# Four-row issue of the second last block's turning transfers, and a later place for the combine weights, in a fused attention and soft-MoE kernel

## The chip, the cores and the metric

The kernel runs on one core of one Trainium2 chip. The metric is device time in microseconds of one execution. Before the change the median of three runs is 650.25 us (649.88 to 651.46). The engines are named as in the profile: PE is TensorE (matmuls; PEld its weight loads), DVE is VectorE, ACT is ScalarE, POOL is GpSimd, and SP is SyncE, which issues the DMA transfers.

## What is computed

The reference is three layers in a row, on 8 sequences of 576 tokens (4608 tokens in all, 512 channels):

```
# 1. attention with a decay per head, 8 heads of 64
scores = (q @ k.T) / 8
x = (scores * Dmat) @ v
# 2. feed-forward, 512 -> 2048 -> 512
h = x @ w_in
x = (h * sigmoid(1.702 * h)) @ w_out
# 3. soft mixture of experts, 8 experts of 4 slots
logits = x @ phi                      # 4608 x 32
d = softmax(logits over the tokens)
slot_input = d.T @ x                  # 32 x 512
slot_out[e] = relu(slot_input[e] @ w1[e]) @ w2[e]
c = softmax(logits over the slots)    # the combine weights
out = c @ slot_out
```

## The kernel before

**Tiling.** The tokens go through in 12 blocks of 384 (n = 0 to 11; LAST is 11). Each block's hidden layer is cut into 16 chunks of 128 (fc = 0 to 15). For one chunk, `expert_scores` (L368) makes the product hp of 12 matmuls; `gelu` (L378) on ScalarE writes the result gT, with the hidden channel on the partitions. The logits never pass through the second feed-forward product: w_out and phi are joined beforehand into Wp, and `logits_group` (L419) multiplies four chunks of gT by it.

**Turning.** The slots' sum needs gT with the token on the partitions. For blocks 0 to 10, VectorE transposes squares of 32 x 32 from gT into pre (L394). SyncE then issues 16 transfers, four rows of four, that put the squares in their places in nat (`shuffle`, L412), once for each half of a block's chunks. A transfer holds 96 KB, in pieces of 1 KB. nat exists once. Block 11 is turned by TensorE in place of this (tpg, L401).

**The softmax over tokens** runs block by block with a running maximum. For block n - 1 it is done during block n: `softmax_split` (L425, L426), `softmax_exp` (product lt, maximum, exponential on ScalarE, L432 to L452), `softmax_turn` (L461: three transposes on TensorE into dp; then VectorE copies dn, finds mx and writes Lall, L463 to L466), and `slots_part` (L479: the product Sg of dn and nat, 12 matmul instructions in the program, 24 in the trace; L485 adds it into acc). Of the twelve products the first two read the first half of nat, the third is the first that reads the second half, and it waits for all transfers of that half. dp stands in the PSUM buffer of tag L, of which there is one; the next block's logits product Lg takes the same buffer, so it waits until L466 has read dp.

**The combine weights.** Lall holds the logits less their maximum, for all tokens. `combine_part(0, NPRE)` takes the exponential of the first 30 of 36 token tiles on ScalarE (L489), and `combine_rest` normalises them with four VectorE instructions (L495 to L498). The other six tiles are done in the tail. The results are read only in the tail.

**The weights of the experts** (w1 and w2, 33.5 MB) and w_out are loaded ahead in the rooms of things that are no longer used: `prefetch` takes the next unit of a fixed list (512 or 1024 KB) and a room, and issues one transfer; `prefetch_three` cuts one room into 1024 and 512 KB. In block 11 a room of tag w (two chunks of w_in) is given away every second chunk, as soon as these chunks' hp product has read it.

**What sets the order.** Everything here is in a `manual_schedule`: each engine runs its instructions in the order in which the code issues them. All transfers stand on SyncE's one queue. They use eight semaphores in turn, so a transfer is issued only when the eighth before it has landed.

Of the kernel before, what the change touches and what calls it, by code (L numbers as in the profile page):

```python
# [9 lines left out]
F32 = mybir.dt.float32  # L10
F32R = mybir.dt.float32r
I32 = mybir.dt.int32
AF = mybir.ActivationFunctionType
# [66 lines left out]
NPRE = NTILE - 2 * NT128  # L80
# [53 lines left out]
def tile_kernel(ctx, tc, qkv, w_in, w_turned, w_out, phi, w1, w2, consts, out):  # L134
    nc = tc.nc
    pe, act, dve, pool, sp = nc.tensor, nc.scalar, nc.vector, nc.gpsimd, nc.sync
# [4 lines left out]
    pw = ctx.enter_context(tc.tile_pool(name="pw", bufs=NFC // 2 - 1, reuse_waits="tile"))  # L141
# [4 lines left out]
    pb = ctx.enter_context(tc.tile_pool(name="pb", bufs=1, side="right", reuse_waits="tile"))  # L146
# [18 lines left out]
    Lall = pp.tile([128, NTILE, NS], F32, name="Lall")  # L165
# [187 lines left out]
    gT, pre, nat, Lg, dn, Lps, dTs = {}, {}, {}, {}, {}, {}, {}  # L353
# [53 lines left out]
    def shuffle(n, hf, rows=range(4)):  # L407
        if n not in nat:
            nat[n] = pm.tile([128, NT128, 4, NFC, 32], F32, tag="nat", name="nat")
        for a in rows:  # L410
            for b in range(4):
                sp.dma_start(nat[n][32 * b:32 * b + 32, :, a, hf * HF:(hf + 1) * HF, :],  # L412
                             pre[n, hf][32 * a:32 * a + 32, :, b])

    def logits_group(n, g):
        if g == 0:
            Lg[n] = ps.tile([128, NB], F32, tag="L", name="Lg")
        for fl in range(GF):
# [38 lines left out]
    def softmax_turn(n):  # L457
        dT = dTs.pop(n)
        dp = ps.tile([128, NT128, 128], F32, tag="L", name="dp")
        for c in range(NT128):  # L460
            pe.transpose(dp[:, c, :], dT[:, c * 128:(c + 1) * 128], ident)  # L461
        dn[n] = pm.tile([128, NT128, NS], F32, tag="dn", name="dn")
        dve.tensor_copy(dn[n], dp[:, :, 0:NS])  # L463
        mx = pm.tile([128, NT128], F32, tag="mx", name="mx")
        dve.tensor_reduce(mx, dp[:, :, NS:2 * NS], axis=AX.X, op=ALU.max)
        dve.tensor_tensor(Lall[:, n * NT128:(n + 1) * NT128, :], dp[:, :, NS:2 * NS],  # L466
                          mx.unsqueeze(2).to_broadcast([128, NT128, NS]), op=ALU.subtract)
# [16 lines left out]
        else:  # L484
            dve.scalar_tensor_tensor(acc, acc, st["corr"], sg, op0=ALU.mult, op1=ALU.add)  # L485

    def combine_part(t0, t1):
        L = Lall[:, t0:t1]
        act.activation(L, L, AF.Exp)  # L489
        combine_rest(t0, t1)  # L490

    def combine_rest(t0, t1):
        L = Lall[:, t0:t1]
        s_ = csum[:, t0:t1]
        dve.tensor_reduce(s_, L, axis=AX.X, op=ALU.add)  # L495
        dve.tensor_scalar(s_, s_, 1e-9, None, op0=ALU.add)
        dve.reciprocal(s_, s_)
        dve.tensor_tensor(L, L, s_.unsqueeze(2).to_broadcast([128, t1 - t0, NS]), op=ALU.mult)  # L498
# [9 lines left out]
    wx, places = {}, []  # L508

    def place_in(pool_, tag, bufs, n=2):  # L510
        return lambda: pool_.tile([128, 1024 * n], F32, tag=tag, name="wx", bufs=bufs)
# [15 lines left out]
    def prefetch(place=None, n=2, lone=False):  # L527
        if not (todo or half_left):
            return
        if place is None:  # L530
            n, place, _ = places.pop(0)
        if lone:
            unit = next(u for u in todo if len(u) == 1)
            todo.remove(unit)
        elif n == 1 and half_left:
            unit = half_left.pop()
        elif n == 1:
            unit = todo.pop(0)
            if len(unit) == 2:
                half_left.append(unit[1:])  # L540
        else:
            pairs_ = [u for u in todo if len(u) == 2]
            unit = pairs_[0] if pairs_ else half_left.pop() if half_left else todo[0]
            if unit in todo:
                todo.remove(unit)
        load_unit(unit[:n], place)
        places.append((n, place, unit[:n]))

    def prefetch_three(t, single, lone=False):

        two = t[:, 1 - single // 2:3 - single // 2].rearrange("p a d -> p (a d)")
        for n in ((1, 2) if single == 0 else (2, 1)):
            prefetch((lambda: t[:, single]) if n == 1 else (lambda: two), n, lone and n == 1)
# [272 lines left out]
    with tc.manual_schedule(engines={getattr(mybir.EngineType, e) for e in ("PE", "Activation", "DVE", "Pool", "SP")}):  # L826
        for x in START:
            step(x)
        for n in range(2, LAST):
            early = n == LAST - 1  # L830
            step_at, logits_at, split_at, exp_at, turn_at, slots_at = (
                (EARLY_STEP_AT, EARLY_LOGITS_AT, EARLY_SPLIT_AT, EARLY_EXP_AT, EARLY_TURN_AT, EARLY_SLOTS_AT) if early else
                (STEP_AT if n < LAST - 2 else BEFORE_EARLY_STEP_AT, LOGITS_AT, SPLIT_AT, EXP_AT, TURN_AT, SLOTS_AT))
            for fc in range(NFC):
                main_fc(n, fc)
                for f in LATE_TURNS.get(fc, (fc,)) if n == 2 else (fc,):
                    turn_fc(n, f)
                if fc in KEEP_AT and n < 2 + NFC // 2 and wide:
                    keep_w_out(2 * (n - 2) + KEEP_AT[fc][0], KEEP_AT[fc][1])

                def between():
                    for m, k in logits_at.get(fc, ()):
                        logits_group(n - m, k)
                    if fc == split_at:
                        softmax_split(n - 1)

                if fc in step_at:
                    step_of((n + 1) * STEPS + step_at[fc], between)
                else:
                    between()  # L850
                if fc == (0 if early else min(step_at)) and (early or n == 2):
                    shuffle(n - 1, 1)
                if early and fc == 2:
                    prefetch(lambda: ring_raw[:, 0:4].rearrange("p a f -> p (a f)"))
                if early and fc == max(step_at):
                    att_ctx.close()
                    pw2 = ctx.enter_context(tc.tile_pool(name="pw2", bufs=NW2, side="right", reuse_waits="tile"))
                    for _ in range(NW2):
                        prefetch(place_in(pw2, "w", NW2))
                if fc == slots_at:  # L860
                    slots_part(n - 1)
                    shuffle(n, 0)
                if fc == exp_at:
                    softmax_exp(n - 1)
                if fc == turn_at:
                    softmax_turn(n - 1)
                if fc == NFC - 1 and not early:
                    if n < LAST - 2:
                        shuffle(n, 1)
                if fc == NFC - 1 and early:  # L870
                    prefetch_three(pb.tile([128, 3, 1024], F32, tag="x", name="wx", bufs=1), 2)
                    shuffle(n, 1)
                    prefetch_three(pb.tile([128, 3, 1024], F32, tag="pre", name="wx", bufs=2), 0)
                if n == 3 and fc == 0:
                    for unit, a in zip(kept, (4, 8)):
                        load_unit(unit, lambda a=a, n=len(unit): ring_raw[:, a:a + 2 * n].rearrange("p a f -> p (a f)"))
        n = LAST
        for fc in range(NFC):
            main_fc(n, fc)
            if fc in LAST_LOGITS:  # L880
                for m, g in LAST_LOGITS[fc]:
                    logits_group(n - m, g)
            if fc == 0:
                softmax_split(n - 1)
            if fc == LAST_EXP_AT:
                softmax_exp(n - 1)
                combine_part(0, NPRE)
            if fc == LAST_TURN_AT:
                softmax_turn(n - 1)
            if fc == LAST_SLOTS_AT:  # L890
                slots_part(n - 1)
            if fc == 5:
                prefetch_three(pb.tile([128, 3, 1024], F32, tag="pre", name="wx", bufs=2), 0, lone=True)
            for f in LAST_TURNS.get(fc, ()):
                turn_fc(n, f)
            if fc == 13:
                prefetch(lambda: gate_room[:, 1536:2560], 1)
            if fc == 0:
                prefetch(place_in(pw, "w1", 2, 1), 1)
            elif fc % 2 == 0:  # L900
                prefetch(place_in(pw, "w", NFC // 2 - 1))
            if fc == GF:
                gate()
                prefetch(lambda: gate_room[:, 0:1024], 1)
        tail()
# [47 lines left out]
```

## Time and profile before

| | us |
|---|---|
| median of three runs | 650.25 |
| the profiled execution's own time | 650.49 |
| its span, first to last instruction | 648.6 |
| TensorE busy | 626.7 (97%) |
| VectorE busy | 293.8 (45%) |
| ScalarE busy | 216.7 (33%) |

The span lies 1.9 us under the execution's own time. Block 10 ends near 532.5 us, block 11 runs from there to about 579, and the tail (the slots' experts and the combination) from there to the end. The granted clock of TensorE is at full speed throughout the blocks. A DMA share is the mean busy share of the core's 16 DMA engines; it can exceed 1 slightly, since packets overlap. A row of the timeline merges neighbouring instructions of one line. "to landing" is the time from a transfer's issue to the moment it is complete on all its engines; the view gives it for some of them.

### The profile page before, as it was taken

To read this page: it belongs to the slowest core of one execution; us is meant where nothing else is said; L and a number is where in the kernel's file an instruction comes from. 1 tells how busy PE (TensorE), PEld (TensorE's weight loads), DVE (VectorE), ACT (ScalarE), POOL (GpSimd) and SP (SyncE) were. 2 spreads that over 40 slices of the span, in tenths; PEclk is the share of its full clock that TensorE was granted. 3 is DMA by queue.
4 is the path that set the end of the run, shared out by engine and by line. 5 is a ranking of instruction groups with operands and counts; after the bars stand their busy time and mean duration, and the time that the engine had idled before them with its cause. 6 is when DMAs were issued, how large, how long until landed. Compare 5 with 4: busy or idle time off the path is not lost.

```text
span 648.6 us, 19162 instructions
## 1 busy us (share of the span) xinstructions
PE 626.7 (97%) x8439; PEld 538.0 (83%) x8439; DVE 293.8 (45%) x581; ACT 216.7 (33%) x409; POOL 77.6 (12%) x70
## 2 busy tenths in 40 slices
PE   6999999999999999999999999999999999999994
PEld 6898788898998989989989979989898798874562
DVE  4989933364453443454534534544535323123043
ACT  2765432141242232422412412412424224231042
POOL 2011101211112101121111011111121100001000
PEclk9999999999999999999999999999999999999997
DMA  8997657687676756746657657566566777999998
GB/s 337 404 329 267 256 109 218 164 215 187 174 265 165 195 187 163 211 141 180 172 163 182 183 145 187 170 158 179 179 176 190 251 204 209 413 361 421 412 414 353
DMA packets 62546, 150.64 MB, mean 232 GB/s; under 512 B 8192, under 2 KB 42368, under 8 KB 53248
## 3 DMA queue, kind: packets, MB, share of 16 engines
q1 hardware_dynamic: 62464, 149.43, 72.8%
q8 instruction: 66, 1.08, 0.7%
q14 instruction: 16, 0.13, 0.1%
HBM read 101.16 MB, written 13.63 MB: 177 GB/s over the span
## 4 chain that ended last, share of the span: by engine, by line
PE 87%; DMA 6%; DVE 3%; ACT 1%; issue 1%; POOL 0%; SPq 0%; DVEq 0%; ACTq 0%
PE hp L368 56%; PE Lg L419 5%; PE Sg L479 4%; PE Sp L227 4%; PE St L227 4%; DMA early_raw<-in_moe_w_in_dram 3%; PE Op L227 2%; PE h_ps L710 2%; PE op L787 2%; PE so_ps L761 1%; DMA early_raw<-in_w_turned_dram 1%; PE so_ps L753 1%; DMA ring<-in_w_turned_dram 1%; DMA pack<-in_qkv_dram 1%; PE tpg L401 1%
## 5 line engine op out<-in xcount | busy, mean ns | idle before, releaser
L368 PE MATMUL hp<-x,w 128*128 128x384 f32 x2304 | 420.0, 339 | 1.6 <-POOL x L257 1.3
L368 PEld LDWEIGHTS hp<-x,w 128*128 128x128 f32 x2304 | 397.4, 188 | 20.2 <-issue 15.7
L394 DVE STREAM_TRANSPOSE pre<-gT 128x384 f32<-128x384 f32 x172 | 95.3, 569 | 165.5 <-ACT gT L378 154.5
L378 ACT ACTIVATE gT<-hp 128x384 f32<-128x384 f32 x188 | 91.1, 490 | 232.6 <-PE hp L368 232.2
L257 POOL TENSOR_TENSOR x<-xs,x 128x512 fp32r<-128x512 f32 x33 | 42.5, 1288 | 310.6 <-ACT x L252 310.6
L227 PE MATMUL Op<-pack 64*64 64x64 f32 x2176 | 71.8, 220 | 0.2 <-issue 0.2
L227 PEld LDWEIGHTS Op<-pack 64*64 64x64 f32 x2176 | 66.8, 135 | 0.6 <-issue 0.6
L252 ACT CAST x<-xs 128x512 fp32r<-128x512 f32 x36 | 22.3, 620 | 87.5 <-DVE xs L245 87.4
L233 POOL TENSOR_TENSOR pack<-pack,cs 128x512 f32<-128x512 f32 x30 | 32.2, 1072 | 126.9 <-DMA pack<-in_qkv_dram 111.3
L227 PE MATMUL Sp<-pack 64*64 64x64 f32 x1152 | 41.3, 222 | 5.6 <-DMA pack<-in_qkv_dram 5.5
L227 PEld LDWEIGHTS Sp<-pack 64*64 64x64 f32 x1152 | 37.8, 138 | 8.1 <-DMA pack<-in_qkv_dram 5.5
L237 DVE TENSOR_TENSOR pack<-Sp,cs 128x512 f32<-128x512 f32 x36 | 24.7, 686 | 33.5 <-PE Op L227 25.8
L227 PEld LDWEIGHTS St<-pack 64*64 64x64 f32 x1024 | 33.2, 137 | 7.4 <-issue 7.3
L227 PE MATMUL St<-pack 64*64 64x64 f32 x1024 | 37.4, 224 | 0.0
L419 PE MATMUL Lg<-gT,Wp 128*32 128x384 f32 x376 | 36.3, 493 | 0.5 <-DVE Lall L466 0.5
L479 PE MATMUL Sg<-nat,dn 128*32 128x512 f32 x264 | 30.4, 593 | 0.0
L245 DVE TENSOR_TENSOR xs<-Op,cs 128x512 f32<-128x512 f32 x36 | 24.5, 681 | 3.1 <-PE Op L227 3.1
L241 DVE TENSOR_TENSOR pack<-St,cs 128x512 f32<-128x512 f32 x32 | 21.8, 680 | 3.4 <-PE St L227 2.0
L304 ACT ACTIVATE early_raw<-early_raw 128x512 f32<-128x512 f32 x28 | 18.9, 685 | 12.3 <-DMA early_raw<-in_moe_w_in_dram 6.3
L479 PEld LDWEIGHTS Sg<-nat,dn 128*32 128x32 f32 x264 | 8.4, 110 | 17.1 <-issue 16.9
L485 DVE SCALAR_TENSOR_TENSOR acc<-acc,corr,Sg 128x512 f32<-128x512 f32 x10 | 7.5, 748 | 28.1 <-PE Sg L479 28.1
L419 PEld LDWEIGHTS Lg<-gT,Wp 128*32 128x32 f32 x376 | 9.6, 109 | 11.9 <-issue 9.1
(142 smaller groups left out, 386.8 us busy)
## 6 DMA issues: line engine op xcount, KB each, us to landing
pack<-in_qkv_dram SPq DMA_DIRECT2D x36, 1024.0 KB, 6.2
nat<-pre SPq DMA_DIRECT2D x352, 96.0 KB, 2.2
wx<-in_moe_w_dram SPq DMA_DIRECT2D x19, 1024.0 KB, 11.2
ring<-in_moe_w_out_dram SPq DMA_DIRECT2D x16, 512.0 KB, 4.0
early_raw<-in_moe_w_in_dram SPq DMA_DIRECT2D x15, 512.0 KB, 6.7
early_raw<-in_w_turned_dram SPq DMA_DIRECT2D x13, 512.0 KB, 6.9
wx<-in_moe_w_dram SPq DMA_DIRECT2D x11, 512.0 KB, 10.1
out_dram<-wx SPq DMA_DIRECT2D x5, 1024.0 KB, 7.5
```

What stands on the lines that cost most here:

```text
L227: pe.matmul(o[oh, p, j, :], w[h, a, p, j], w[h, b, p, j], start=first_, stop=True, skip_group_check=True)
L233: (dve if n in (3, 4) else pool).tensor_tensor(k, k, by_state(ksc[:, n % NPB, :]), op=ALU.mult)
L237: dve.tensor_tensor(packs[n][:, SC], Sps.pop(n), across(dtab), op=ALU.mult)
L241: dve.tensor_tensor(packs[n][:, SS], St[n // NPB], by_state(stsc[:, n % NPB, :]), op=ALU.mult)
L245: dve.tensor_tensor(xss[g], Ops.pop(g), across(osc), op=ALU.mult)
L252: act.copy(xh[b_][:, :, i * CP:(i + 1) * CP], xss[g].rearrange("p a j c -> p a (j c)"))
L257: (eng or pool).tensor_tensor(xl[b_][:, :, cols_], xss.pop(g).rearrange("p a j c -> p a (j c)"), xh[b_][:, :, cols_], op=ALU.subtract)
L368: pe.matmul(hp, wt[fc][:, a, dc, :], b[n][:, dc, :], start=(i == 0), stop=(i == 3 * NDC - 1))
L378: act.activation(gT[n, g][:, fl, :], hps.pop((n, fc)), AF.Gelu_apprx_sigmoid)
L394: dve.transpose(pre[n, hf][:, :, :, fh, :].rearrange("p c b i -> p (c b) i"), gT[n, g][:, fl, :].rearrange("p (x j) -> p x j", j=32))
L419: pe.matmul(Lg[n][32 * fl:32 * fl + 32, :], Wp[:, g * GF + fl, :], gT[n, g][:, fl, :], start=(g == 0), stop=(g == NFC // GF - 1))
L479: pe.matmul(Sg[32 * b:32 * b + 32], dn[n][:, c, :], nv[:, 4 * b:4 * b + 4], start=(c == 0), stop=(c == NT128 - 1))
```

## The change

1. At the end of block 10, the sixteen turning transfers of its second half were issued in one go, between two weight loads and three others. Now they are issued row by row, four transfers each, and behind each of the first three rows stands one of the weight loads that followed before: 512 KB and 1024 KB into the room of the block's first half of pre, and 512 KB into the room of w_in's first chunk. The last of these was issued behind chunk 0 of block 11. The units and their order in the list of weights stay the same.
2. In block 11, ScalarE's exponential of the combine weights stays behind `softmax_exp`, but the four VectorE instructions of `combine_rest` come behind `softmax_turn` in place of ahead of it. `combine_part` is gone.

```diff
@@ block 10, last chunk
                     prefetch_three(pb.tile([128, 3, 1024], F32, tag="x", name="wx", bufs=1), 2)
-                    shuffle(n, 1)
-                    prefetch_three(pb.tile([128, 3, 1024], F32, tag="pre", name="wx", bufs=2), 0)
+                    room = pb.tile([128, 3, 1024], F32, tag="pre", name="wx", bufs=2)
+                    shuffle(n, 1, [0])
+                    prefetch(lambda: room[:, 0], 1)
+                    shuffle(n, 1, [1])
+                    prefetch(lambda: room[:, 1:3].rearrange("p a d -> p (a d)"))
+                    shuffle(n, 1, [2])
+                    prefetch(place_in(pw, "w1", 2, 1), 1)
+                    shuffle(n, 1, [3])
@@ block 11
             if fc == LAST_EXP_AT:
                 softmax_exp(n - 1)
-                combine_part(0, NPRE)
+                act.activation(Lall[:, 0:NPRE], Lall[:, 0:NPRE], AF.Exp)
             if fc == LAST_TURN_AT:
                 softmax_turn(n - 1)
+                combine_rest(0, NPRE)
...
-            if fc == 0:
-                prefetch(place_in(pw, "w1", 2, 1), 1)
-            elif fc % 2 == 0:
+            if fc and fc % 2 == 0:
                 prefetch(place_in(pw, "w", NFC // 2 - 1))
```

On SyncE's queue, from the weights at the end of block 10 on, the order before is this (L412 are turning transfers, L523 weight loads, 128x2048 is 1024 KB and 128x1024 is 512 KB; gT is a weight load into the room of gT):

```order
L523 DMA wx<-in_moe_w_dram 128x2048
L523 DMA wx<-in_moe_w_dram 128x1024
L412 DMA nat<-pre 32x3x256 x16
L523 DMA wx<-in_moe_w_dram 128x1024
L523 DMA wx<-in_moe_w_dram 128x2048
L523 DMA wx<-in_moe_w_dram 128x1024
L523 DMA wx<-in_moe_w_dram 128x2048 x2
L523 DMA gT<-in_moe_w_dram 128x1024
```

The same stretch of the changed kernel, where the weight loads are line 518:

```order
L518 DMA wx<-in_moe_w_dram 128x2048
L518 DMA wx<-in_moe_w_dram 128x1024
L412 DMA nat<-pre 32x3x256 x4
L518 DMA wx<-in_moe_w_dram 128x1024
L412 DMA nat<-pre 32x3x256 x4
L518 DMA wx<-in_moe_w_dram 128x2048
L412 DMA nat<-pre 32x3x256 x4
L518 DMA wx<-in_moe_w_dram 128x1024
L412 DMA nat<-pre 32x3x256 x4
L518 DMA wx<-in_moe_w_dram 128x2048 x2
L518 DMA gT<-in_moe_w_dram 128x1024
```

Three weight loads moved up, one in front of each of the last three rows of turning transfers.

On VectorE, in block 11 between the end of `softmax_exp` (L452) and the sum of the slots (L485), the difference is this:

```order
 L452 COPY dT<-lt 32x384
-L495 TENSOR_REDUCE csum<-Lall 128x30
-L496 TENSOR_SCALAR csum<-csum 128x30
-L497 RECIPROCAL csum<-csum 128x30
-L498 TENSOR_TENSOR Lall<-Lall,csum 128x960
-L463 COPY dn<-dp 128x96
-L465 TENSOR_REDUCE mx<-dp 128x3
-L466 TENSOR_TENSOR Lall<-dp,mx 128x96
+L463 COPY dn<-dp 128x96
+L465 TENSOR_REDUCE mx<-dp 128x3
+L466 TENSOR_TENSOR Lall<-dp,mx 128x96
+L490 TENSOR_REDUCE csum<-Lall 128x30
```

The three readers of dp (L463 to L466) now stand ahead of the four combine instructions (L490 to L493 in the new numbering).

## Rows read from the trace of the kernel before

**Rows 1.** The page: busy time of the engines, and DMA share in 40 slices.

```profile
PE 626.7 (97%) x8439; PEld 538.0 (83%) x8439; DVE 293.8 (45%) x581; ACT 216.7 (33%) x409; POOL 77.6 (12%) x70
DMA  8997657687676756746657657566566777999998
```

**Rows 2.** Timeline of TensorE in block 11: start, duration, instructions, idle time before.

```profile
542.92 0.49 PE L461 MATMUL dp<-ident,dT 128*128 128x128 f32 x3
543.16 2.33 PE L368 MATMUL hp<-x,w 128*128 128x384 f32 x12
545.98 0.85 PE L419 MATMUL Lg<-gT,Wp 128*32 128x384 f32 x8 [0.49 <-DVE Lall L466]
...
551.13 2.78 PE L479 MATMUL Sg<-nat,dn 128*32 128x512 f32 x24
```

**Rows 3.** Stretches: PE, PEld, DVE, ACT, POOL busy (count); clock, DMA share, GB/s.

```profile
539.00:541.00 2.00, 2.00 (x14) 2.00 (x13) 0.75 (x3) 1.97 (x5) 0.00 (x0) 1.00 1.07 269
546.00:548.00 2.00, 2.00 (x15) 1.38 (x16) 0.00 (x0) 0.08 (x1) 0.00 (x0) 1.00 0.63 134
554.00:560.00 6.00, 6.00 (x44) 5.36 (x43) 1.84 (x3) 1.69 (x4) 0.00 (x0) 1.00 1.01 417
577.00:578.00 1.00, 1.00 (x7) 1.00 (x7) 0.00 (x0) 0.22 (x1) 0.00 (x0) 1.00 1.01 180
578.00:580.00 2.00, 2.00 (x16) 1.09 (x14) 0.56 (x1) 1.13 (x2) 0.00 (x0) 1.00 0.77 315
620.00:645.00 25.00, 18.99 (x324) 12.48 (x316) 12.13 (x24) 11.10 (x28) 0.00 (x0) 0.92 1.01 414
```

**Rows 4.** Waits of SyncE's queue from 552.9 to 600: total us, times, longest.

```profile
SPq L523 <- PE hp L368: 12.9, 3, 4.5
```

**Rows 5.** Timeline of SyncE's queue, 515 to 600.

```profile
532.81 1.03 SPq L523 DMA_DIRECT2D wx<-in_moe_w_dram  x2
533.94 13.22 SPq L412 DMA_DIRECT2D nat<-pre  x16
547.21 3.79 SPq L523 DMA_DIRECT2D wx<-in_moe_w_dram  x5
...
576.66 3.40 SPq L523 DMA_DIRECT2D wx<-in_moe_w_dram  x4
```

**Rows 6.** Timelines at the end: last rows of TensorE and of SyncE's queue.

```profile
638.68 1.34 PE L787 MATMUL op<-dT,acc 32*128 32x128 f32 x12
640.69 1.14 SPq L797 DMA_DIRECT2D out_dram<-wx  x1
```

**Rows 7.** Timelines of VectorE and ScalarE in block 11.

```profile
542.17 1.15 DVE L495 TENSOR_REDUCE csum<-Lall 128x30 f32<-128x960 f32 x1
...
545.12 0.26 DVE L463 COPY dn<-dp 128x96 f32<-128x96 f32 x1
...
545.58 0.26 DVE L466 TENSOR_TENSOR Lall<-dp,mx 128x96 f32<-128x96 f32 x1
553.98 0.75 DVE L485 SCALAR_TENSOR_TENSOR acc<-acc,corr,Sg 128x512 f32<-128x512 f32 x1 [8.14 <-PE Sg L479]
543.45 0.88 ACT L378 ACTIVATE gT<-hp 128x384 f32<-128x384 f32 x2
```

**Rows 8.** Transfers: weight issued 533.4; packets 539 to 541; turning, last, all, first seven.

```profile
L523 SPq DMA_DIRECT2D wx<-in_moe_w_dram x2: 450/495/540, 532.8 to 533.4; - x2
wx<-in_moe_w_dram SPq DMA_DIRECT2D x1, 512.0 KB, 7.7
DMA packets 546, 0.54 MB, mean 269 GB/s; under 512 B 78, under 2 KB 527, under 8 KB 546
DMA to landing us min/median/max: 3.4/3.4/3.4
DMA to landing us min/median/max: 2.2/3.2/8.7
DMA to landing us min/median/max: 7.2/7.2/7.2
```

More of the change, by code (lines that the diff above doesn't have):

```diff
@@ L485, in slots_part @@
             dve.scalar_tensor_tensor(acc, acc, st["corr"], sg, op0=ALU.mult, op1=ALU.add)
[L487 to L490, printed above, removed]
     def combine_rest(t0, t1):
```

## Prediction

> **What bounds the kernel now.** I read the page's busy shares first [rows 1]: TensorE is busy 97% of the span of 648.6 us, and the DMA line stays at 9 from the last sixth on. So there are two candidates, and the place of the change lies where one hands over to the other. The timeline of TensorE in the last block [rows 2] then shows its only pause near the change: the logits product at 545.98 waits 0.49 us for VectorE's write of Lall (L466). The product Sg at 551.13 waits for nothing.
>
> The DMA side is read in stretches [rows 3]. While the sixteen turning transfers go out alone the engines are not full (share 0.63 at 546 to 548); from 554 on they run at about 417 GB/s. At 577 to 580 they falter (180 GB/s, then a share of 0.77), and behind that they are full again (1.01 from 620 to 645). SyncE's waits [rows 4] say why: behind 552.9 it waits 12.9 us in three waits for hp products to set weight rooms free. The room of chunks 13 and 14 is free only at 576.66 [rows 5], when the queue has run dry. After that the queue is never empty: TensorE's last matmuls end at 640.02, the last output transfer is issued at 640.69, and the span lasts 8 us more [rows 6]. So the end is set by TensorE up to the release at 576.66 and by the DMA stream behind it. Whatever moves TensorE's time at 576.66 moves the end by as much; what the queue gains before 576.66 is lost there.
>
> **Part 1, the combine work.** In the trace VectorE does L495 to L498 from 542.17 to 545.12, 2.95 us, and only then L463 to L466, from 545.12 to 545.84 [rows 7]. Their input, the three transposes dp, ends at 542.92 + 0.49 = 543.41 [rows 2]. With the order turned, L463 to L466 take the same 0.72 us from about 543.45 and end at 544.2. The logits product may then start when the hp product in front of it ends, 543.16 + 2.33 = 545.49, instead of 545.98: **0.49 us gained on TensorE**. Next late at that place is the gelu of chunk 3, done at 543.45 + 0.88 = 544.33 [rows 7], 1.2 us early, so nothing gives the gain back there. The four combine instructions now run from 544.2 to 547.2. Their cover is VectorE's idle time of 8.14 us up to 553.98 [rows 7]; without it they would cost 2.95 us in front of the next VectorE step. Their results are read in the tail alone. The exp on ScalarE keeps its place: nothing.
>
> **Part 2, the transfers.** Nothing is added: the same sixteen turning transfers and three weight loads (512, 1024 and 512 KB) are issued, on the one queue, SyncE's. Before, the sixteen went first, 533.94 to 547.16, and the weights followed from 547.21 [rows 5]. Now one weight load stands behind each of the first three rows. Who waits for the last turning transfer: Sg, whose third product of twelve needs the second half of nat. The last one, whose issue of 0.6 us ends the sixteen's row at 547.16 [rows 5], went out at 546.6 and landed 3.4 us later, at 550.0 [rows 8], so Sg at 551.13 had about 1.2 us to spare. Behind Sg on TensorE stands everything else.
>
> When is the last row there now? The two weight loads in front are unchanged. Of the second one only 546 - 527 = 19 packets are left after 539.0 [rows 8]; from there the queue is full. In the two microseconds that follow, 527 - 78 = 449 packets of 1 KB pass [rows 8]; at 96 packets, one turning transfer takes 96 / 225 = 0.43 us, sixteen take 6.8 us. The three weights, 2.1 MB at 417 GB/s [rows 3], take 5.0 us. Together 11.8 us: 550.8 if all engines ran level. They don't: the 512 KB load issued at 533.4 landed 7.7 us later, at 541.1 [rows 8], so its slowest engine was 2.1 us behind; and the last turning transfer landed 3.4 us after issue where the quickest took 2.2, a lag of 1.2 us. A landing counts when the slowest engine is done, so 550.8 + 1.2 = 552.0 to 550.8 + 2.1 = 552.9; I take the middle, **552.5**. The issue is not later than that: a transfer is issued only when the eighth before it has landed, so the fifteenth waits for the 1024 KB load, on the slowest engine 541.1 + 8 x 0.43 + 1.25 + 2.5 = 548.3; the sixteenth follows 0.6 us later and with 2.2 us of landing gives 551.1.
>
> Bounds: from below, 550.8, no lag at all. From above, a pause each time the stream turns from turning packets to weights. That operation isn't in the trace with a full queue; the nearest row is 577 to 578, where new weights move 180 instead of 417 GB/s, 0.57 us lost. Three times that on the slow engine gives 552.9 + 1.7 = 554.6. I take no pause, since the three loads are issued well before their turn and the row is one of an emptied queue.
>
> Sg without the wait would start at 551.13 - 0.49 = 550.64. Two of its twelve products (2.78 us in all, 0.23 each, partly overlapping [rows 2]) go ahead of the wait and save some 0.1. Its end moves by 552.5 - 551.13 - 0.1 = **+1.3 us** against before: 1.8 us of new wait, 0.5 us of gain. With the bounds it is -0.4 to +3.4. From 553.84 to 576.66 TensorE has no pause that could absorb it, so the release moves by 1.3 us, and the DMA stream behind it too.
>
> Here the order in the queue decides. The row first: of the seven turning transfers issued behind the two weights from 533.9 on, the one whose landing the view gives took 7.2 us against 2.2 for the quickest [rows 8]. The Trainium skill ("DMA: Bandwidth & Descriptors", Queues, rings and completion order) states that on each DMA engine descriptors are consumed in ring order, and this trace agrees; by it the fourth row cannot land before the three weights are through. If turning transfers could pass weights, the last would land near 550.0 as before, and the sum would be -0.5 instead of +1.3.
>
> Sum: 650.49 us for the profiled execution, + 1.3 = 651.8; that execution lies 0.24 us over the median of 650.25, so on the median 651.55, rounded **651.6 us**.
>
> **The rivals.**
> (a) The fourth row lands early enough (up to 551.4, lag gone): Sg hardly waits, and the end moves by -0.5 to +0.2: 649.8 to 650.4, say 650.0. For it: 550.8 on level engines. Against it: a slow engine in each weight load of these rows.
> (b) The other side, slower by over 0.3%: the pauses do come, and the landing is at 553.2 or later. Three pauses of 0.57 us on a lag between the two put it at 553.7 to 554.6, 554.1 in the middle; the end moves by 554.1 - 551.2 = +2.9: 653.1. For it: the falter at 577 [rows 3], and that the landing needs all engines. Against it: from 539 to 541, with the queue full, the share is 1.07, with no pause as weights gave way to turning packets. It decides from a landing of 553.2.
> (c) The stream gain lasts. Before, the three weights could be through at the earliest at 550.0 + 5.0 = 555.0, now with the last row at 552.5: the queue is 2.5 us ahead. If the end hung on the stream alone from 554 on, it would come 2.5 us earlier: 647.8. For it: shares of 1.01 from 554 to 560 and from 620 to 645 [rows 3]. Against it: the 12.9 us in which SyncE waits for rooms, and the dry queue at 577 to 580. The Trainium skill ("DMA: Bandwidth & Descriptors", Rules for kernel authors) advises to issue a DMA early and to wait for it late, which points this way; in this trace the rooms are the limit, not the issue.
> **How the numbers follow.** Forecast (landing 551.4 to 553.2, end +0.2 to +2.0): 0.55. (a) 0.14, (b) 0.26, (c) 0.05. A measurement of this kernel can tell some 0.3%, 1.95 us, from no change. Faster by that: (c) alone, 0.05. Slower by that: (b), 0.26. Within: the forecast and (a), 0.69. The range leaves out (c) and the upper half of (b): 649.6 (the whole gain of part 1 with little wait) to 653.1.
>
> **What would show it.** In the changed kernel: no wait of the logits product behind dp, which starts about 0.5 us earlier (545.5); Sg with a wait for nat's transfers of 1 to 2.5 us; a DMA share near 1 from 546 to 548 where it was 0.63; the dry stretch before the release at 576.66 longer, not gone; the release itself about 1.3 us later, and the stretch from there to the end as long as before. The prediction is wrong if Sg starts without a wait (the queue is faster than 225 packets/us), or if the stretch from the release to the end gets shorter.

## The result, and the profile after

The changed kernel takes **656.03 us** (median of 6 runs, 655.53 to 657.48), the kernel before 649.91 in the same comparison: a ratio of 1.0095 (95% interval 1.0079 to 1.0111), 6.1 us more. The prediction was 651.6 us, with a range of 649.6 to 653.1 and a chance of 0.26 on slower by over 0.3%: the time lies outside the range, on the slow side.

The profiled execution takes 656.04 us, its span 654.2. Block 11 starts up to 2 us earlier or later from one execution to the next (532.76 to 534.72 in the twelve traces of this document), so the times below are counted from **M**, the start of the block's first logits product, which groups 2 and 3 of block 10 form: 534.72 before, 534.00 after. From M to the span's end it is 113.91 us before and 120.15 after, **+6.24 us** to explain.

TensorE in block 11 of the changed kernel (start, duration, idle time ahead in brackets), to be read beside [rows 2]:

```profile
542.20 0.49 PE L461 MATMUL dp<-ident,dT 128*128 128x128 f32 x3
542.45 2.33 PE L368 MATMUL hp<-x,w 128*128 128x384 f32 x12
544.71 0.85 PE L419 MATMUL Lg<-gT,Wp 128*32 128x384 f32 x8
...
549.87 1.05 PE L479 MATMUL Sg<-nat,dn 128*32 128x512 f32 x4
555.01 4.16 PE L479 MATMUL Sg<-nat,dn 128*32 128x512 f32 x20 [4.09 <-DMA nat<-pre]
```

Lg starts at M + 10.71 without a wait, where it was M + 11.26 with one. Sg starts as early as foreseen, M + 15.87; its first four instructions, which read the first half of nat, run, and then it waits until 555.01 = M + 21.01 (before: M + 16.87). And the other twenty instructions take 4.16 us, where before all twenty-four took 2.78. The reason for that second loss is in stretches of 1 us (TensorE busy and its instructions, granted clock, DMA share, GB/s):

```profile
553.00:554.00 1.00, 0.00 (x0) 1.00 0.98 342
554.00:555.00 1.00, 0.00 (x0) 0.72 0.96 393
555.00:556.00 1.00, 0.99 (x8) 0.50 1.04 434
556.00:557.00 1.00, 1.00 (x12) 0.50 0.99 414
557.00:558.00 1.00, 1.00 (x8) 0.57 0.97 393
558.00:559.00 1.00, 1.00 (x8) 1.00 1.03 414
```

While TensorE stood idle its granted clock fell from full (2.4 GHz) to 0.50 (1.2 GHz), and Sg ran at that level for the first 2.8 us after its data came. In the kernel before the clock stays full throughout these blocks.

SyncE's queue over the same time, and its waits for hp behind 552.9 (those of before: [rows 4, 5]):

```profile
533.21 2.56 SPq L412 DMA_DIRECT2D nat<-pre  x4
535.87 0.56 SPq L518 DMA_DIRECT2D wx<-in_moe_w_dram  x1
536.47 4.79 SPq L412 DMA_DIRECT2D nat<-pre  x4
...
545.59 3.98 SPq L412 DMA_DIRECT2D nat<-pre  x4
549.67 1.02 SPq L518 DMA_DIRECT2D wx<-in_moe_w_dram  x2
...
554.86 21.58 SPq L518 DMA_DIRECT2D wx<-in_moe_w_dram  x6
577.30 0.33 SPq L518 DMA_DIRECT2D gT<-in_moe_w_dram  x1
581.91 3.40 SPq L518 DMA_DIRECT2D wx<-in_moe_w_dram  x4
```
```profile
SPq L518 <- PE hp L368: 17.3, 3, 8.7
```

The last turning transfer goes out near 548.5, and by the trace's landing events its slowest engine is done at 554.71 = M + 20.71, the median engine at M + 18.51. The room of chunks 13 and 14 is released at 581.91 = M + 47.91 (before M + 41.94): 5.97 us later, as much as the end of Sg (M + 25.17 against M + 19.20). Longest of SyncE's waits is now 8.7 us where it was 4.5: the queue, ahead of TensorE, stands still for longer. The stretches, for [rows 3] (busy times of the five engines, then clock, DMA share, GB/s):

```profile
546.00:548.00 2.00, 2.00 (x13) 2.00 (x12) 0.28 (x1) 0.05 (x1) 0.00 (x0) 1.00 1.14 276
554.00:560.00 6.00, 4.99 (x28) 1.92 (x29) 0.75 (x1) 0.32 (x1) 0.00 (x0) 0.72 1.01 412
568.00:572.00 4.00, 4.00 (x28) 3.92 (x27) 0.56 (x1) 1.55 (x4) 0.00 (x0) 1.00 0.26 109
572.00:576.00 4.00, 4.00 (x25) 3.73 (x23) 0.56 (x1) 0.67 (x2) 0.00 (x0) 1.00 0.72 262
620.00:645.00 25.00, 23.97 (x434) 15.92 (x426) 11.30 (x22) 11.32 (x28) 0.00 (x0) 1.00 1.01 415
```

The hole of 546 to 548 (share 0.63 before) is filled, and what was gained there is lost at 568 to 576, as predicted. The end, for [rows 6]: TensorE's last matmuls and the last output transfer.

```profile
643.92 1.34 PE L782 MATMUL op<-dT,acc 32*128 32x128 f32 x12
645.94 1.14 SPq L792 DMA_DIRECT2D out_dram<-wx  x1
```

From the release to the span's end it is 72.24 us (before 71.96). On the page the busy time of TensorE rises from 626.7 us [rows 1] to 629.6; this Sg is 2.4 of it (1.05 + 4.16 against 2.78):

```profile
PE 629.6 (96%) x8439; PEld 539.4 (82%) x8439; DVE 295.1 (45%) x581; ACT 217.3 (33%) x409; POOL 77.6 (12%) x70
```

And VectorE, for [rows 7]: dn is copied as soon as dp is there, the combine work follows behind Lall, and the idle time that was its cover has grown to 12.93 us.

```profile
542.73 0.26 DVE L463 COPY dn<-dp 128x96 f32<-128x96 f32 x1 [1.38 <-PE dp L461]
...
543.18 0.26 DVE L466 TENSOR_TENSOR Lall<-dp,mx 128x96 f32<-128x96 f32 x1
543.36 1.14 DVE L490 TENSOR_REDUCE csum<-Lall 128x30 f32<-128x960 f32 x1
...
559.21 0.75 DVE L485 SCALAR_TENSOR_TENSOR acc<-acc,corr,Sg 128x512 f32<-128x512 f32 x1 [12.93 <-PE Sg L479]
```

### The profile page after: what moved, and what is told of

Same layout as the page of the kernel before. It is cut to its first block, busy times and chain, and to the rows that moved or that the text cites. A ratio compares the mean times of both kernels' runs of the same rounds, so it can differ in the third digit from the quotient of the medians.

```text
span 654.2 us, 19161 instructions
## 1 busy us (share of the span) xinstructions
PE 629.6 (96%) x8439; PEld 539.4 (82%) x8439; DVE 295.1 (45%) x581; ACT 217.3 (33%) x409; POOL 77.6 (12%) x70
## 4 chain that ended last, share of the span: by engine, by line
PE 86%; DMA 8%; DVE 2%; ACT 1%; issue 1%; SPq 0%; POOL 0%; DVEq 0%; ACTq 0%
PE hp L368 55%; PE Lg L419 5%; PE Sg L479 5%; PE Sp L227 4%; PE St L227 4%; DMA early_raw<-in_moe_w_in_dram 3%; PE Op L227 3%; PE h_ps L705 2%; DMA wx<-in_moe_w_dram 2%; PE op L782 2%; PE so_ps L756 1%; PE so_ps L748 1%; DMA nat<-pre 1%; DMA early_raw<-in_w_turned_dram 1%; DMA pack<-in_qkv_dram 1%; PE tpg L401 1%
## 5 line engine op out<-in xcount | busy, mean ns | idle before, releaser
L479 PE MATMUL Sg<-nat,dn 128*32 128x512 f32 x264 | 33.4, 616 | 4.1 <-DMA nat<-pre 4.1
L485 DVE SCALAR_TENSOR_TENSOR acc<-acc,corr,Sg 128x512 f32<-128x512 f32 x10 | 7.5, 748 | 30.9 <-PE Sg L479 30.9
```

The costliest lines, as they stand in the source:

```text
L479: pe.matmul(Sg[32 * b:32 * b + 32], dn[n][:, c, :], nv[:, 4 * b:4 * b + 4], start=(c == 0), stop=(c == NT128 - 1))
```

## The experiments

**The theory.** The end of Sg sets the time. It is late for two reasons: the last turning row lands later than the weights in front of it should make it by their own durations, and the pause that this causes costs the clock. Rivals: the weights' bytes alone explain the landing; the clock's fall is a companion and costs nothing; or the end hangs on the DMA stream, and not on Sg. In the experiments' texts the landing is that of the second half's last turning transfer, on its slowest engine.

The median time of each run and its ratio to the kernel before (650.1 to 650.2 us beside them, 649.91 beside the changed kernel; the ratio, with its 95% interval, is close to that of the two medians but not the same), and three times of its one profiled execution, counted from M; all in us:

| run | time | ratio (95%) | landing | end of Sg | span's end |
|---|---|---|---|---|---|
| before | 650.2 | 1 | 15.25 | 19.20 | 113.91 |
| after | 656.03 | 1.0095 (1.0079 to 1.0111) | 20.71 | 25.17 | 120.15 |
| e1 combine only | 648.98 | 0.9986 (0.9972 to 1.0000) | 14.73 | 18.65 | 113.48 |
| e2 transfers only | 654.95 | 1.0072 (1.0046 to 1.0099) | 19.76 | 24.53 | 119.51 |
| e3 filler | 653.45 | 1.0052 (1.0036 to 1.0068) | 19.87 | 22.94 | 117.67 |
| e4 covered | 650.20 | 0.9996 (0.9982 to 1.0009) | 20.18 | 25.89 | 113.65 |
| e5 one between | 649.28 | 0.9997 (0.9980 to 1.0013) | 15.12 | 18.65 | 113.58 |
| e6 two between | 651.96 | 1.0023 (1.0006 to 1.0039) | 16.96 | 19.93 | 114.67 |
| e7 weights first | 652.87 | 1.0042 (1.0029 to 1.0055) | 18.42 | 21.58 | 116.30 |
| e8 late turns | 650.44 | 1.0003 (0.9987 to 1.0020) | 14.33 | 18.65 | 114.37 |
| e9 late turns and loads | 649.11 | 0.9984 (0.9971 to 0.9998) | 14.46 | 18.65 | 113.22 |
| e10 the same, one between | 648.57 | 0.9976 (0.9963 to 0.9990) | 14.94 | 18.65 | 113.11 |

**The two halves of the change (e1, e2).** e1 is the kernel before with `combine_rest` behind `softmax_turn`; e2 is the changed kernel with it put back:

```
             if fc == LAST_EXP_AT:
                 softmax_exp(n - 1)
                 act.activation(Lall[:, 0:NPRE], Lall[:, 0:NPRE], AF.Exp)
+                combine_rest(0, NPRE)
             if fc == LAST_TURN_AT:
                 softmax_turn(n - 1)
-                combine_rest(0, NPRE)
```

Expected of e1:

> The kernel before with the moved VectorE work alone; the transfers stay as they were. Theory 1 (the whole loss of the changed kernel comes from Sg's wait for the last row and from the slow clock behind it): the logits product starts without its wait, 0.5 us earlier, Sg waits for nothing, and the end comes 0.5 us earlier, 649.4 us where before has 649.9. Rival (the moved work itself costs something): slower than before, by up to its 2.9 us, with a new wait on VectorE behind dp.

Expected of e2:

> The changed kernel with the combine work back at its old place; the four rows with weights between them stay. Theory 1: the landing of the last row sets the end of Sg, whoever comes early only waits longer, so the time is that of the changed kernel, 656.0 us, with Sg waiting 3.6 us in place of 4.1. Rival (the two parts add up): 656.5 to 656.6 us.

e1 has Lg at M + 10.71 and its span's end 0.43 us earlier. By time it is 0.14% faster, at the edge of what the interval allows. Part 1 does what the prediction said, no more. All the loss is in the transfers, with the wait (2.60 us, where 3.6 was expected), the half clock and the late row seen again. Sg in e2, then the clock:

```profile
552.83 4.46 PE L479 MATMUL Sg<-nat,dn 128*32 128x512 f32 x20 [2.60 <-DMA nat<-pre]
```
```profile
552.00:553.00 1.00, 0.17 (x4) 1.00 0.97 401
553.00:554.00 1.00, 1.00 (x8) 0.53 1.06 442
554.00:555.00 1.00, 1.00 (x8) 0.50 0.98 410
555.00:556.00 1.00, 1.00 (x9) 0.50 0.97 397
556.00:557.00 1.00, 1.00 (x8) 0.76 1.01 406
```

Here the clock falls only after Sg has gone on, behind a pause of 2.60 us. The two kernels' ratios overlap; that the changed kernel, which has part 1's gain as well, isn't quicker than e2 goes with its row landing 0.95 us later in that execution, and why it did stays open.

**The clock by itself (e3).** The changed kernel, with 24 matmuls whose result nobody reads ahead of Sg, so that TensorE stays busy while the transfers land:

```
             if fc == LAST_SLOTS_AT:
+                t = ps.tile([128, NB], F32, tag="h", name="again", bufs=3)
+                for i in range(24):
+                    pe.matmul(t, wt[fc][:, 0, i % NDC, :], xh[n][:, i % NDC, :], start=True, stop=True)
                 slots_part(n - 1)
```

> The changed kernel with 24 more matmuls (128 x 384, results unused) in front of Sg, about 4.2 us of TensorE work in the time in which it waits. Theory 1: the wait shrinks to some 0.5 us at full clock, the granted clock doesn't fall, the twenty late products of Sg take 2.3 us in place of 4.2, and the time falls by 1.8 us to 654.2 us, though there is more work. Rival (Sg is slow because its data or the memory is busy, not because of the clock): Sg still takes 4.2 us behind the landing and the time stays at 656.0 us.

```profile
549.08 4.33 PE L895 MATMUL again<-x,w 128*128 128x384 f32 x24
553.34 2.92 PE L479 MATMUL Sg<-nat,dn 128*32 128x512 f32 x24
```
```profile
553.34:556.26 2.92, 2.92 (x26) 1.00 0.99 412
```

Work added, and the kernel is 2.6 us faster than the changed one (653.45 against 656.03). The clock stays at 1.00, and not in this trace alone: over a whole execution it is 0.994 to 0.996 in all eight runs of e3, and 0.990 to 0.992 in all six of the changed kernel. From the row's landing to Sg's end it takes 3.07 us (M + 19.87 to 22.94) in place of 4.46 (20.71 to 25.17), so **the fall of the clock cost 1.4 us**, and it did cost; the other 0.8 us is a row that landed at M + 19.87 and not at 20.71. The expectation had 1.8 us for the clock, since it took 2.3 us for the twenty instructions at full clock; behind a wait they take 2.77 (e7, below). The DMA engines are as full as in the changed kernel while Sg runs (share 0.99), so it was not their load that slowed it there. The late row alone, with full clock, leaves the kernel 0.52% slower.

**The wait covered (e4).** The changed kernel with the hp products of chunks 7 to 9 ahead of Sg, and the turns of block 11, with the gelu of chunks 8 and 9, moved behind it to make room (the gelu's lines are left out here):

```
-LAST_TURNS = {6: (0, 1), 7: (2, 3), 8: (4, 5), 9: (6, 7), 10: (8,), 11: (9,), 12: (10,), 13: (11,)}
-LAST_EXP_AT, LAST_TURN_AT, LAST_SLOTS_AT = 1, 3, 6
+LAST_TURNS = {9: (0, 1, 2, 3), 10: (4, 5), 11: (6, 7), 12: (8, 9), 13: (10, 11)}
+LAST_EXP_AT, LAST_TURN_AT, LAST_SLOTS_AT = 1, 3, 9
...
```

> The changed kernel with the hp products of chunks 7, 8 and 9 of the last block ahead of Sg (6.3 us of work), and block 11's turns of chunks 0 to 3 behind Sg; the same work in another order. Theory 1 (TensorE sets the end up to the release of the room of chunks 13 and 14, so the queue's lead is lost there): no wait at Sg, full clock, release 0.5 us earlier than before, 649.4 us. Rival (the lead of the queue lasts, as in rival c of the prediction): the end comes 2 to 2.5 us earlier than that, 647 us.

```profile
555.51 2.37 PE L368 MATMUL hp<-x,w 128*128 128x384 f32 x12
557.80 2.78 PE L479 MATMUL Sg<-nat,dn 128*32 128x512 f32 x24
```

The row is as late as ever (M + 20.18), but Sg does not wait, and the whole loss is gone: 0.9996. Neither is there a gain, although the queue is ahead by all three weight loads. So the damage goes through Sg alone, and the lead is worth nothing here.

**How the landing grows (e5 to e7).** Only the first 512 KB between the rows (e5); the 512 KB behind row 1 and the 1024 KB behind row 2 (e6); all three loads ahead of row 1 (e7). The edit of e5, of which the other two are variants:

```
                     shuffle(n, 1, [0])
                     prefetch(lambda: room[:, 0], 1)
-                    shuffle(n, 1, [1])
+                    shuffle(n, 1, [1, 2, 3])
                     prefetch(lambda: room[:, 1:3].rearrange("p a d -> p (a d)"))
-                    shuffle(n, 1, [2])
                     prefetch(place_in(pw, "w1", 2, 1), 1)
-                    shuffle(n, 1, [3])
```

> The changed kernel with only the first weight load (512 KB) between the rows, behind row 1; the other two follow behind row 4. Times of the landing are counted from the start of the last block's first logits product (16 matmuls), where the last row lands at 15.2 us before and at 20.0 to 20.7 us in the changed kernel and in the runs with its transfers so far. Theory 2 (every load in front of the last row costs its own time in the queue, 1.3 to 1.5 us for 512 KB and 2.5 to 2.7 us for 1024 KB, beyond what the issue of the turning transfers leaves free): landing at 15.5 to 16.2 us, Sg waits up to 0.5 us, 649.5 to 650.2 us. Rival (a single change between turning packets and weights already costs most of the 5 us): landing from 18 us on, over 652 us.

> The changed kernel with two weight loads between the rows (512 KB behind row 1, 1024 KB behind row 2); the third follows behind row 4. Theory 2: landing at 18.0 to 18.8 us, Sg waits 2 to 3 us; 651.5 us if the clock stays, 653.3 us if it falls to the lower level. Rival (the last load of 512 KB is the one that hurts, since the fifteenth and sixteenth transfers are held back by the eight in flight): landing at 17 us or before, under 651 us.

> The changed kernel with all three weight loads ahead of row 1 and the sixteen turning transfers in one go behind them: the same bytes in front of the last row, one change from weights to turning packets in place of three and back. Theory 2a (the landing is late because of the alternation: first weight packets behind turning packets are slow, and turning packets slow beside weights): landing at 18 to 18.6 us, some 2 us earlier than in the changed kernel, 651.5 to 653.5 us. Theory 2b (only the bytes and packets ahead count, each slower than taken): landing at 20 to 20.7 us as in the changed kernel, 655 to 656 us.

On its slowest engine the row lands at M + 14.7 without weights (e1), then at 15.1, 17.0 and about 20 (19.8 to 20.7): the first load costs 0.4 us, the second 1.8, the third about 3, though its 512 KB are worth 1.25 us at 417 GB/s. Bytes alone don't do that. On the median engine it looks otherwise: M + 13.9, 15.0, 16.0 and 17.9 to 18.5, so 4.1 to 4.6 us for the three loads, less than the 5.0 us that their bytes take at that rate. The expectations of e5 (15.5 to 16.2) and e6 (18.0 to 18.8) were too late. e6 lands where its rival had it, but its time is not under 651, and the rule of eight that this rival names does not hold back the last row of the changed kernel: there the last transfer is issued 4.1 us before the median engine lands it, before the change 2.1 us. e7 has the same bytes in front of the last row and lands at M + 18.42 with all its engines together (median M + 18.34), as its theory 2a had it, but it isn't a clean counterpart: its turning transfers are held back by the rule of eight, and the last goes out only at M + 16.24.

What can be read is that in the changed kernel and its variants e2 to e4 the median engine (17.9 to 18.5) lands about when e7's does, and the slowest one 1.8 to 2.2 us behind the median. With no weights between the rows that lag is 0.6 to 1.25 us (before, e1, e8, e9), with one load 0.1 us (e5, e10), with two 1.0 us (e6), so it does not simply follow the loads. Towards the end of the rows it grows at one place in all twelve traces: a packet of 16 KB of instruction code (q8 on the page) passes, and the lag of the transfers that land behind it jumps by 0.4 to 1.6 us (in e5, e7 and e10 it is gone again before the last transfer). Before, the packet lies at M + 12.2 to 13.7 and the lag goes from 0.1 to 1.6 us, without any weights there; in the changed kernel it lies at M + 13.9 to 15.2, and the lag goes from 0.7 to 2.2 us. The packet in both (546.85 to 548.45 before, 547.8 to 549.2 after; packets, MB, share of 16 engines):

```profile
q8 instruction: 1, 0.02, 5.9%
```
```profile
q8 instruction: 1, 0.02, 5.9%
```

The packet's own time, 1.5 and 1.3 us in these two, would account for most of the lag. These traces don't say which engine is the slow one, and no run moves the packet, so this is a likely cause and not a shown one; whether rows and weights in turn spread the engines apart as well stays open.

e7 also bounds the clock: a wait of 1.89 us without a fall. Behind it, at full clock, Sg's twenty instructions take 2.77 us, as long as all twenty-four before.

```profile
548.91 1.05 PE L479 MATMUL Sg<-nat,dn 128*32 128x512 f32 x4
551.86 2.77 PE L479 MATMUL Sg<-nat,dn 128*32 128x512 f32 x20 [1.89 <-DMA nat<-pre]
```
```profile
551.86:554.63 2.77, 2.77 (x21) 1.00 0.91 384
```

The starts in the traces show why. Before, the twenty-four begin in six rounds of four, 0.43 us apart; in e7 the twenty begin in six rounds too, of 4, 4, 4, 4, 2 and 2, since two of the four products that run side by side have not begun ahead of the wait. e6 gives 2.77 us behind a wait of 0.24. So the price of the half clock is 4.16 - 2.77 = 1.4 us in the changed kernel, as e3 has it, and 4.46 - 2.77 = 1.7 us in e2.

The profiled executions of e6 and e7 are the quickest of ten each, 2.0 and 1.6 us under their medians, so their medians hold something that these traces don't show. It isn't the clock alone: of these twenty runs only three show a clock under 0.994 over the whole execution. It stays open.

**What sets the end (e8 to e10).** The prediction had the DMA stream set the end behind the release of the room of chunks 13 and 14. e8 is e1 with the turns of chunks 8 to 11, the third logits group and one weight load of 512 KB moved towards chunk 15, so that this room comes free earlier (the load's lines are left out here):

```
-LAST_LOGITS = {0: ((1, 2), (1, 3)), 4: ((0, 0),), 8: ((0, 1),), 12: ((0, 2),)}
-LAST_TURNS = {6: (0, 1), 7: (2, 3), 8: (4, 5), 9: (6, 7), 10: (8,), 11: (9,), 12: (10,), 13: (11,)}
+LAST_LOGITS = {0: ((1, 2), (1, 3)), 4: ((0, 0),), 8: ((0, 1),), 15: ((0, 2),)}
+LAST_TURNS = {6: (0, 1), 7: (2, 3), 8: (4, 5), 9: (6, 7), 14: (8, 9), 15: (10, 11)}
...
```

> The kernel before with the moved VectorE work alone, and in the last block the turns of chunks 8 to 11 and the logits of these chunks behind the product of chunk 14, with the 512 KB weight load that needs their room behind chunk 15: 2.1 us of TensorE work moves from ahead of the release of the room of chunks 13 and 14 to behind it. Theory 1 (the end is the release plus a stream of fixed length): the release comes 2 us earlier and so does the end, 647 us. Rival (the end hangs on TensorE's work in the tail, which has as much to do as ever, or the stream is not fixed): 649 us as with the moved VectorE work alone, or later.

The release came 2.35 us earlier (M + 39.05 against e1's 41.40), and the span's end 0.9 us *later*: the queue now faltered behind it, at the rooms that come next.

```profile
573.00:574.00 1.00, 1.00 (x9) 1.00 (x8) 0.56 (x1) 0.56 (x2) 0.00 (x0) 1.00 0.73 246
574.00:575.00 1.00, 1.00 (x7) 1.00 (x6) 0.00 (x0) 0.00 (x0) 0.00 (x0) 1.00 0.70 229
577.00:578.00 1.00, 1.00 (x12) 0.21 (x10) 0.76 (x2) 0.98 (x2) 0.00 (x0) 1.00 0.51 143
```

e9 goes on from there: all four turns at 15, and two loads that wait for no room behind them (512 and 1536 KB) kept back for that time. e10 is e9 with e5's first load between the rows. From e9's edit:

```
+            if fc == NFC - 1:
+                prefetch(place_in(pw, "w1", 2, 1), 1)
+                prefetch_three(pg.tile([128, 3, 1024], F32, tag="x", name="wx", bufs=1), 2)
             for f in LAST_TURNS.get(fc, ()):
                 turn_fc(n, f)
...
```

> Part 2 undone, the combine work moved, and the order at the end of the last block changed: the turns of chunks 8 to 11 and the third logits group come behind the hp product of chunk 15, and so do two weight loads of the list (512 KB into w_in's first chunk, 1536 KB into x's room of block 10), which until then are not put into the queue at the end of block 10. The hp products of chunks 13 to 15 come earlier by what stood between them, so the room of chunks 13 and 14 is given away earlier. Theory (the end hangs on the last stretch in which SyncE's queue has run dry for want of a room): e1_combine_only still loses some 1.4 us at its release, from M + 40 to M + 43 (M is the start of the last block's first logits product), where shares of 0.95, 0.52 and 0.57 stand; here the queue is not dry behind M + 15, and the span ends near M + 112.1, 647.6 us. Rival (the next room in the list gates it in turn, as the room of chunk 15 did in e8_late_turns): the queue still falters, only at another place, span end M + 113.5 to M + 114.5, 649 to 650 us.

> e9_late2 with the first 512 KB weight load of the changed kernel behind the first row of turning transfers, as in e5_one_between (where the last row landed at M + 15.1, and nothing waited for it). Theory (a lead of the queue counts once no room gates it any more): the 512 KB are ahead for good, so the span ends up to 1.25 us before that of e9_late2, M + 110.9, 646.4 us. Rival (a room behind it gates all the same): the same time as e9_late2 within 0.3 us.

e9's end falls between its two expectations; e10's is that of e9 within 0.11 us, as the rival had it, but no room is the reason. By its shares e9's queue loses 0.3 us at the rooms, e1's 1.1, and yet e9's span ends only 0.26 us before e1's, and e10's, with 1.25 us of loads more behind it, 0.37. These are single traces, and the medians of e1, e5, e9 and e10 (648.98, 649.28, 649.11, 648.57) with their overlapping intervals put the kernels in no sure order; that the gain is far under the lead is what they show. Where the lead went shows at the handover from the last weights to the first output, 84 to 88 us behind M; the rows are of before, e1, e9 and e10 in this order:

```profile
618.72:622.72 4.00, 4.00 (x80) 2.51 (x76) 1.59 (x3) 1.73 (x4) 0.00 (x0) 1.00 1.01 410
```
```profile
617.57:621.57 4.00, 4.00 (x76) 2.32 (x67) 2.12 (x4) 1.97 (x4) 0.00 (x0) 1.00 0.96 391
```
```profile
618.42:622.42 4.00, 4.00 (x70) 2.42 (x64) 2.38 (x4) 2.15 (x4) 0.00 (x0) 1.00 0.95 387
```
```profile
618.21:622.21 4.00, 4.00 (x68) 2.42 (x64) 2.38 (x4) 2.15 (x4) 0.00 (x0) 1.00 0.91 372
```

The further the queue is ahead, the emptier it is here: the weights are through and the first output isn't computed. It is issued at M + 87.39, 86.85, 86.60 and 86.59. TensorE is busy all four microseconds, and its waits between 570 us and the end are short and for other engines, never for a DMA; that holds in before, e1, e8, e9, e10 and in the changed kernel, of which the longest three are

```profile
PE sr_ps L766 <- ACT gT L761: 0.7, 1, 0.7
PE tps L669 <- DVE acc L655: 0.6, 1, 0.6
PE dr L626 <- ACT Lp L621: 0.5, 1, 0.5
```

From the issue of the first output to the span's end it is 26.5 to 26.8 us in eleven of the twelve traces, whatever the queue did ahead of it (28.0 in e8).

So two chains run side by side from block 11 to the outputs, TensorE's work and the DMA stream, and they are about equally long. A delay of TensorE in block 11 lengthens both, since the stream waits for rooms that TensorE frees. A gain of the stream shortens one.

e10 has the lowest median, 648.57 us, 0.24% under the kernel before (interval 0.10 to 0.37%) and 1.1% under the changed one. It keeps the combine move and one of the three weight loads.

## Why the prediction was wrong

**Part 1: right.** 0.49 us predicted, 0.55 measured at Lg; nothing gave it back (e1: Sg ends 0.55 us earlier, the span 0.43). The combine work found its cover in VectorE's idle time.

**The path: right as far as the release.** Sg's third product waits for the last row, and Sg's end moves TensorE's later work: Sg's end moved by 5.97 us, the release by 5.97, the span's end by 6.24. e4 shows it from the other side. What the prediction hung on the release alone is the last point below. The Trainium skill ("DMA: Bandwidth & Descriptors", Queues, rings and completion order), which the prediction quoted, states that each DMA engine consumes descriptors in ring order. The last rows behind three weights, at M + 18.4 to 20.7 against 14.3 to 15.25 behind none, agree.

**The landing: the term that was mis-sized.** The prediction took 552.5, with M = 534.72 that is M + 17.8, and 554.6 = M + 19.9 as its upper bound. The five runs with all three loads between rows or ahead of them gave 18.4 to 20.7, the changed kernel's own trace 20.7: **2.9 us** more than the point. Counted on its median engine, the two loads in front are through at M + 5.1, where the prediction counted from M + 4.3 (+0.8); a turning transfer takes 0.48 us and not 0.43 (16 of them: +0.9); the three weights take 5.7 us and not 5.0 (+0.7); and the slowest engine lags by 2.2 us where 1.7 stood (+0.5). The durations had come from stretches in which one kind of packet had the queue nearly to itself; for the mixture there was no row. The lag of 1.2 us had come from the kernel before, where the packet of instruction code lies just ahead of the last landing too. The bound from above, three pauses, was thereby too narrow as well. Rival (b), given one chance in four, had the direction; its price, 2.9 us, was short too, and its mechanism is not seen: in every microsecond from 539 to 553 the mean DMA share is 0.96 to 1.27, so the engines as a whole made no pause.

**The clock: the term that was missing.** The prediction let Sg wait 1.8 us and then run on at full speed. Its upper bound of 554.6 implied a pause near 4 us, and the price of such a pause on the products behind it was not asked. By the rows it is 1.4 us in the changed kernel (4.16 for what takes 2.77), and e3 gives 1.4 back. The Trainium skill ("TensorE: Matmul & The Clock Gate", Why this matters for your kernels) warns that idle gaps between matmul bursts throw the clock back to its lower level. The changed kernel and e2, each with such a gap, agree; e3, without one, kept its clock, and e7's gap of 1.89 us went without a fall.

Two small terms were wrong with it: Sg's third product starts 0.3 us behind the last engine's landing, and the two products ahead of the wait save nothing where 0.1 us stood, 0.4 us in all. Landing, clock and these, 2.9 + 1.4 + 0.4 = 4.7 us on the predicted +1.3, give 6.0 of the 6.24 us.

**The stream's lead: right that it is lost, half right why.** Rival (c) fell in e4 and e5. But "the end is set by the DMA stream behind the release" was only one half: e9 and e10 kept the stream fuller and hardly gained, because TensorE's chain to the first output is as long; and in e8 the release came 2.35 us earlier without moving the end forward.

## What to carry to other kernels

A transfer that TensorE waits for should not be queued behind loads that nobody waits for, unless the waiting product can be moved behind other work: filling a hole in the queue cost 6 us here, and the covered form of the same queue cost none. When a change puts a wait of some microseconds in front of TensorE, ask whether the clock falls in it and add that price (1.4 to 1.7 us here), or fill the pause. And before a lead of the DMA queue is booked as a gain, look for the next place where it runs dry: a full queue with a product chain of the same length beside it gave back tenths of a microsecond here.

## What was unexpected of the hardware

The granted clock fell behind a pause of 2.60 us (e2, there only after the work had resumed) and one of 4.09 us, and not behind 1.89 us (e7): the fall need not show in the pause itself. With turning packets of 1 KB and weight packets in one queue, the DMA share was full (1.14 from 546 to 548, at 276 GB/s) and yet a transfer of 96 KB took 0.48 us in place of 0.43. In every trace the slowest engine's lag behind the median one jumped, by 0.4 to 1.6 us, behind one 16 KB packet of instruction code, in the kernel before as well; that the packet is the cause is likely and not shown. And a product of twelve parts, of which two could go ahead of the wait, took as long behind it as the whole (2.77 and 2.78 us).
